# Clustered attention with a max-out FFN on one Trainium2 core: preparations and weight conversion pinned to fixed score tiles, raw weights loaded ahead, value products in one run

## The chip, the cores and the metric

The kernel runs on one core of a Trainium2 chip. Five engines work from queues of their own, each strictly in the order in which its instructions were written: TensorE (PE, matmuls; PEld are its weight loads), VectorE (DVE), ScalarE (ACT), GpSimd (POOL) and SyncE (SP), which here issues every DMA. The metric is device microseconds of one execution. Three runs of the kernel before took 872.66, 874.25 and 877.45 us; the median is 874.25 us.

## The reference

Two steps follow each other. The first is attention that is allowed only inside a cluster, for 4 batches, 8 heads, 768 positions and a head width of 64:

```
q_assign = argmax(q_n @ c_n.T)          # 16 centroids per head, normalised
k_assign = argmax(k_n @ c_n.T)
scores   = q @ k.T / sqrt(64)
scores   = where(q_assign == k_assign, scores, -1e9)
attn     = exp(scores - max) / (sum + 1e-9)
x        = attn @ v                     # then 3072 tokens x 512
h        = max(x @ w1, x @ w2, x @ w3)  # 512 -> 768
out      = h @ w_out                    # 768 -> 512
```

The inputs of the attention are float32 and the four weight matrices are float64. The kernel keeps about float32 accuracy from 16-bit matmuls: an operand is scaled by a power of two and split into a high and a low float16 half, and a product is three matmuls (high by high, high by low, low by high).

## The kernel before, in words

**Tiles.** A *score tile* is 128 query positions of one head against all 768 keys. A batch has 8 heads of 6 tiles, so 48 tiles, and the whole kernel 192, numbered 0 to 191 here. Two heads make a pair (4 pairs a batch), and three tiles of both heads of a pair make a *visit* of six tiles; after the four visits of one half of the queries (24 tiles) come those of the other half.

**One score tile** (`scores`): PE multiplies queries and keys into one of three PSUM buffers `big` (L482 and L484; the second also adds the mask, carried as 32 extra rows of the operands). DVE scales it and takes the row extreme (L487). ACT takes the exponential (L490) and casts it to float16 (L493). The low half is a subtraction (L495), by DVE on even tiles and by POOL on odd ones. On an even tile the whole sequence works in the PSUM buffer, so that the buffer comes free only after the subtraction of DVE; on an odd tile it is free after the exponential. SP then issues a transposing DMA `pt<-hl` (L496).

**One visit** ends with `av`: 6 small matmuls spread the row sums (L510), 36 matmuls of 64 output columns multiply the transposed tiles `pt` with the values (L514), ACT copies the row sums, DVE multiplies (L524, L526), POOL splits the result `x` (L528, L529).

**The FFN** of each half batch (`ffn_units`) has 18 groups of 12 matmuls (L555) and 3 groups of 18 (L589), spread over the 24 tiles that follow. The last half batch has no tiles after it.

**Preparations.** For each pair `prep_units` gives six units: load of two heads, scales, split, cluster scores on PE, moves by DMA, and the argmax with the mask rows on DVE (L434 to L465). `v_prep` splits the values of a pair; batch 0 takes them from two large loads (`v_max_first`), later batches load them inside `v_prep` (L333).

**Weights.** They are float64 in memory. `convert` takes one of two buffers `wd`, loads 512 KB of raw bits (L195), lets ACT cast the high part (L197) and DVE join the low part (L199). There are 18 such pieces for w1, w2, w3 and 6 for w_out, all in batch 0. `split16` then makes the halves. Each load is held back by a tiny POOL copy (`hold`, L120) into the buffer, which reads the row sum of the newest tile.

**What sets the order.** The order of each engine is fixed when the program is built. Every unit gets a priority (`at_prio`), mostly the number of the tile beside which it should stand; a scheduler then fills each engine's queue with a timeline of its own and takes, among what it believes ready, the lowest priority. So a unit whose inputs the scheduler believes ready early is drawn forward into any gap of its timeline. `behind` ties a unit's instructions to one earlier instruction of the same engine; `spread` distributes units over a stretch of tiles.

## Time and profile before

The profiled execution took 872.91 us; its span, from the first to the last instruction, is 871.1 us.

| stretch | us | what is in it |
|---|---|---|
| 0 to 24.8 | 24.8 | start, centroids, preparation of pair 0 |
| 24.8 to 256.6 | 231.8 | tiles 0 to 47: batch 0, all weights |
| 256.6 to 452.2 | 195.6 | tiles 48 to 95: batch 1 |
| 452.2 to 635.9 | 183.7 | tiles 96 to 143: batch 2 |
| 635.9 to 804.8 | 168.9 | tiles 144 to 191: batch 3, nothing left to prepare |
| 804.8 to 871.1 | 66.3 | the last FFN |

The stretches are cut where L487 of tiles 0, 48, 96, 144 and 191 starts. Over the span PE is busy 84%, DVE 64%, ACT 53% and POOL 52%. A matmul's busy time overlaps that of the next one, so that the spacing of starts says what it costs. A timeline row gives the start, the duration, the engine, the line and the tiles, and in brackets how long the engine stood idle before it and what ended that. A row of waits gives the engine and line that waited, for what, the total in us, how many times and the longest.

### The profile page before, as it was taken

To read this page: it belongs to the slowest core of one execution; us is meant where nothing else is said; L and a number is where in the kernel's file an instruction comes from. 1 tells how busy PE (TensorE), PEld (TensorE's weight loads), DVE (VectorE), ACT (ScalarE), POOL (GpSimd) and SP (SyncE) were. 2 spreads that over 40 slices of the span, in tenths; PEclk is the share of its full clock that TensorE was granted. 3 is DMA by queue.
4 is the path that set the end of the run, shared out by engine and by line. 5 is a ranking of instruction groups with operands and counts; after the bars stand their busy time and mean duration, and the time that the engine had idled before them with its cause. 6 is when DMAs were issued, how large, how long until landed. Compare 5 with 4: busy or idle time off the path is not lost.

```text
span 871.1 us, 13288 instructions
## 1 busy us (share of the span) xinstructions
PE 729.3 (84%) x4629; PEld 391.6 (45%) x4629; DVE 559.7 (64%) x1169; ACT 463.1 (53%) x827; POOL 450.4 (52%) x464
## 2 busy tenths in 40 slices
PE   2035374788868989999789999997999999999997
PEld 0012132344434545555444555454545554555563
DVE  7663877786897867547686686368768663556110
ACT  2545467654663646646554656464556465566201
POOL 1166355658585565337655745266666652354221
PEclk9976566689888999999999999999999999999999
DMA  6176869986786778768888978597986976666300
GB/s 230 36 169 140 201 143 214 203 182 139 178 204 128 171 167 154 138 117 165 170 157 201 188 139 142 113 180 144 189 194 128 156 136 134 112 118 110 91 1 36
DMA packets 329154, 128.90 MB, mean 148 GB/s; under 512 B 304384, under 2 KB 315520, under 8 KB 329088
## 3 DMA queue, kind: packets, MB, share of 16 engines
q1 hardware_dynamic: 329088, 128.06, 71.5%
q8 instruction: 36, 0.59, 0.3%
q14 instruction: 30, 0.25, 0.1%
HBM read 31.49 MB, written 6.29 MB: 43 GB/s over the span
## 4 chain that ended last, share of the span: by engine, by line
PE 45%; DVE 18%; POOL 11%; DMA 10%; issue 9%; ACT 5%; SPq 1%; POOLq 0%; DVEq 0%; ACTq 0%
PE one L555 17%; PE one L589 11%; PE big L514 7%; DVE big L487 4%; PE big L482 4%; PE big L484 3%; POOL hl L495 3%; DMA pt<-hl 2%; DMA stage<-in_qk_dram 2%; PE big L510 2%; DMA wd<-in_moe_w_dram 2%; DMA wd<-in_moe_w_out_dram 2%; POOL qk L399 2%; DMA stage<-in_v_dram 2%; DVE hl L495 2%
## 5 line engine op out<-in xcount | busy, mean ns | idle before, releaser
L487 DVE TENSOR_SCALAR_CACHE_REDUCE big<-big,nsc 128x768 f32<-128x768 f32 x192 | 194.2, 1017 | 78.3 <-PE big L484 77.1
L495 POOL TENSOR_TENSOR hl<-e,hl 128x768 f16<-128x768 f32 x96 | 159.0, 1656 | 148.9 <-ACT hl L493 147.3
L555 PE MATMUL one<-x,w16a 128*128 128x384 f16 x1152 | 208.1, 330 | 5.1 <-DVE vf_h L567 3.7
L490 ACT ACTIVATE big<-big,nm 128x768 f32<-128x768 f32 x96 | 83.8, 873 | 146.3 <-DVE big L487 130.9
L555 PEld LDWEIGHTS <-w16a 128*128 128x128 f16 x1152 | 111.1, 98 | 90.0 <-issue 21.1
L482 PE MATMUL big<-qk 128*128 128x512 f16 (+1 forms) x384 | 105.9, 357 | 48.5 <-DVE hl L495 14.0
L514 PE MATMUL big<-pt,v 128*64 128x384 f16 x1152 | 129.8, 341 | 2.4 <-DMA pt<-hl 2.4
L490 ACT ACTIVATE e<-big,nm 128x768 f32<-128x768 f32 x96 | 86.5, 901 | 71.3 <-DVE big L487 56.4
L495 DVE TENSOR_TENSOR hl<-big,hl 128x768 f16<-128x768 f32 x96 | 91.4, 952 | 41.8 <-ACT hl L493 39.6
L555 PE MATMUL one<-x,w16b 128*128 128x384 f16 x576 | 108.3, 340 | 6.7 <-DVE vf_h L567 5.2
L484 PE MATMUL big<-qk 96*128 96x512 f16 (+1 forms) x384 | 106.5, 357 | 6.9 <-DVE qk L465 4.3
L514 PEld LDWEIGHTS <-v 128*64 128x64 f16 x1152 | 71.8, 114 | 50.9 <-issue 26.0
L482 PEld LDWEIGHTS <-qk 128*128 128x128 f16 x384 | 35.6, 102 | 104.8 <-issue 67.2
L493 ACT CAST hl<-e 128x768 f16<-128x768 f32 x96 | 80.1, 834 | 2.4 <-DMA pt<-hl 0.6
L555 PEld LDWEIGHTS <-w16b 128*128 128x128 f16 x576 | 57.5, 101 | 51.3 <-issue 17.5
L493 ACT CAST hl<-big 128x768 f16<-128x768 f32 x96 | 76.6, 798 | 2.0
L528 POOL TENSOR_SCALAR x<-xs 128x384 f16<-128x384 f32 x32 | 16.4, 512 | 99.3 <-DVE xs L524 83.8
L484 PEld LDWEIGHTS <-qk 96*128 96x128 f16 x384 | 40.4, 105 | 40.0 <-issue 9.2
L589 PE MATMUL one<-wo,wf_h 128*128 128x512 f16 x216 | 56.0, 381 | 0.8 <-ACT o L598 0.8
L589 PE MATMUL one<-wo,vf_h 128*128 128x512 f16 x216 | 51.8, 380 | 2.7 <-DVE vf_h L567 2.4
L367 DVE TENSOR_REDUCE q_m<-stage 128x1 f32<-128x768 f32 x32 | 30.2, 948 | 33.9 <-DMA stage<-in_qk_dram 33.8
L399 POOL TENSOR_TENSOR qk<-stage,qk 128x768 f16<-128x768 f32 x30 | 49.6, 1667 | 3.1 <-ACT qk L398 2.9
(150 smaller groups left out, 892.5 us busy)
## 6 DMA issues: line engine op xcount, KB each, us to landing
stage<-in_qk_dram SPq DMA_DIRECT2D x32, 384.0 KB, 5.0
wd<-in_moe_w_dram SPq DMA_DIRECT2D x18, 512.0 KB, 4.8
out_dram<-o SPq DMA_DIRECT2D x24, 256.0 KB, 2.5
qk<-qk SPq DMA_DIRECT2D x15, 384.0 KB, 4.3
qk<-qk SPq DMA_DIRECT2D x30, 192.0 KB, 3.4
stage<-in_v_dram SPq DMA_DIRECT2D x12, 384.0 KB, 4.6
pt<-hl SPq DMA_TRANSPOSE x192, 4.0
wd<-in_moe_w_out_dram SPq DMA_DIRECT2D x6, 512.0 KB, 4.5
```

The costliest lines, as they stand in the source:

```text
L367: nc.vector.tensor_reduce(m2[:, i : i + 1], x, axis=AX.X, op=ALU.max, apply_absolute_value=True)
L399: last["lo"] = nc.gpsimd.tensor_tensor(t[:, AQ, i], x, t[:, BQ, i], op=ALU.subtract)
L482: nc.tensor.matmul(t[:, lo:hi], aq[:, qs], ak[:, lo:hi], start=True, stop=False)
L484: last["pe"] = nc.tensor.matmul(t[:, lo:hi], bq[0:K2, qs], bk[0:K2, lo:hi], start=False, stop=True)
L487: last["nm"] = nc.vector.tensor_scalar(e, e, nsc[b, h // 2], 3.0e38, op0=ALU.mult, op1=ALU.min, accum_out=nm)
L490: nc.scalar.activation(x, e, AF.Exp, bias=nm, scale=-1.0, accum_out=r)
L493: nc.scalar.copy(hl[:, 0, :], x)
L495: eng.tensor_tensor(hl[:, 1, :], x, hl[:, 0, :], op=ALU.subtract)
L510: nc.tensor.matmul(t[D * i : D * i + D, at : at + P], w, ident, start=True, stop=True)
L514: nc.tensor.matmul(t[D * i : D * i + D, 0:NB], v[:, i, kt, a], pts[i][:, :, c * QT + kt, :], start=(n == 0), stop=(n == len(parts) - 1),)
L555: nc.tensor.matmul(t[:, 0:NB], w16[jt // JA][:, jt % JA, wa, i, ct], x16[b, gi, ct][:, xa, :], start=(n == 0), stop=(n == 3 * CT - 1),)
L589: nc.tensor.matmul(t[:, 0:DM], h16[jt][:, ha, tt * P : (tt + 1) * P], wo16[0][:, jt, wa, :], start=(n == 0), stop=(n == 3 * JT - 1),)
```

## The change

Seven edits go together.

- `convert` becomes `w_load` (the DMA) and `w_convert` (ACT and DVE). The `hold` copies on POOL go.
- The 24 raw loads, conversions and splits get fixed tiles: piece n is converted at 1.9 n − 0.8 and loaded two tiles before that; before, they were spread over three stretches.
- `paced` is new: all instructions of a unit are tied behind the newest score matmul (PE), scaling (DVE), exponential (ACT), subtraction (POOL) and transposition (SP) at the point where the plan places it. Preparations, values and weights all go through it, and the raw loads of the later batches' values (`v_load`) stand two tiles ahead of their use.
- The value products are paced too, with a priority five tiles ahead of their place. `AV_LAG` goes from 2 to 3, and what follows the products (`x_split`) is a unit of its own one tile later.
- The two large value loads of batch 0 are issued at the start, and both their maxima are taken beside tiles, not before tile 0.
- `v_prep` of batch 0 stands at tiles 3, 9, 15 and 21.
- The FFN's 18 groups start one tile later in each half batch.

```
+    def w_load(wp, src, a, n):
         x = wp.tile([P, n + 1, 4], I16, tag="wd", name="wd", bufs=2)
-        hold(x[0:1, 0, 0:2].bitcast(F32))
         xf = x.rearrange("p n w -> p (n w)")
         nc.sync.dma_start(out=xf[:, 1 : 1 + 4 * n].rearrange("p (a m) -> p a m", a=a), in_=src)
+        return x
+
+    def w_convert(x, d):
...
-        nc.scalar.activation(x, e, AF.Exp, bias=nm, scale=-1.0, accum_out=r)
-        pace[:] = [r[0:1]]
+        last["exp"] = nc.scalar.activation(x, e, AF.Exp, bias=nm, scale=-1.0, accum_out=r)
...
+        if by_pool:
+            last["pool"] = i
...
+    def paced(step, u, late=-1):
+
+        def f():
+            with ExitStack() as st:
+                for k in ("pe", "nm", "exp", "pool", "dma"):
+                    if k in last:
+                        st.enter_context(tc.issue_after(last[k].ins))
+                u()
+
+        plan.setdefault(max(int(step // 1), 0), []).append((step + late, f))
...
-    behind("lo", vm[0])
+    wl[0]()
     first[5]()
...
-    spread([lambda u=u: behind("nm", u) for u in prep_units(0, 1)], 0, 3, -4)
-    spread([lambda u=u: behind("nm", u) for u in vm[1:]] + [lambda: v_prep(0, 0, True)], 0, 4, 0)
-    spread(prep_units(0, 2), 4, 9, -4)
-    spread(prep_units(0, 3), 10, 15, -4)
+    W_STEP = 1.9
+    for n in range(24):
+        k = 2 + (n - 2) * W_STEP
+        if n >= 2:
+            paced(k - 1, (wl + ol)[n])
+        paced(max(k + 1, 0.5), (wc + oc)[n])
+        if n < 18 and n % 3 == 2:
+            for i, u in enumerate(wu[n // 3][2]):
+                paced(k + 2 + i, u)
+    paced(47, w_common)
+    for k, u in zip((0, 1, 2, 2, 3), p1[1:]):
+        paced(k, u)
+    for k in (2, 3, 4):
+        paced(k - 1, vm[k])
+    prep_at(0, 2, (3, 5, 6, 7, 8, 9))
+    prep_at(0, 3, (9, 11, 12, 13, 14, 15))
+    for pr in range(NPAIR):
+        paced(V * pr + 3, lambda pr=pr: v_prep(0, pr, True))
...
-    spread(wa[W_0:], *W_A, W_LATE)
-    spread([u for j in range(JA, JT) for u in w_units(fp[0], j)], *W_B, W_LATE)
-    spread(wo_units(fp), *W_O, W_LATE)
...
-                t = at + HS + V + 7.5 * pr
-                spread(prep_units(b + 1, pr), t + 1, t + 10, PREP_LATE)
-                t = at + nsteps + (-14, -8, -2, 3)[pr]
-                spread([lambda b=b, pr=pr: v_prep(b + 1, pr)], t, t)
+                t = at + 28 + 9 * pr
+                prep_at(b + 1, pr, (t, t + 2, t + 3, t + 5, t + 6, t + 7))
+                t = at + nsteps + (-13, -7, -1, 3)[pr]
+                paced(t - 2, lambda b=b, pr=pr: v_load(b + 1, pr))
+                paced(t, lambda b=b, pr=pr: v_prep(b + 1, pr))
...
-                spread([u for j in h for u in j], k + 3, k + HS, F_LATE)
+                spread([u for j in h for u in j], k + 4, k + HS, F_LATE)
...
-        u = lambda a=(b, pr, gi, pts, rs): behind("pe", av, *a)
-        plan.setdefault(step + AV_LAG - 1, []).append((step + AV_LATE, u))
+        paced(step + AV_LAG - 1, lambda a=(b, pr, gi, pts, rs): av(*a), -5)
+        paced(step + AV_LAG, lambda a=(b, pr, gi): x_split(*a))
```

The queues of the built programs show three places. Line numbers move with the change: L482, L484, L490, L493, L496, L510, L514, L555, L195 and L197 become L498, L500, L506, L508, L513, L528, L532, L577, L186 and L193.

On PE, a value product of batch 1 (`v_2390` is the split values of pair 3). Before, the products stand between the matmuls of the FFN's output (L589):

```order
L510 MATMUL big<-ident,rs 64x128
L589 LDWEIGHTS wf_h
L589 MATMUL one<-wo_1015,wf_h 128x512
L514 LDWEIGHTS v_2390
L514 MATMUL big<-pt,v_2390 64x384
L589 LDWEIGHTS wf_h
L589 MATMUL one<-wo_1015,wf_h 128x512
```

The same product (there `v_2364`) after the change:

```order
L577 MATMUL one<-x_3086,w16a 128x384
L528 MATMUL big<-ident,rs 64x128 x6
L532 LDWEIGHTS v_2364
L532 MATMUL big<-pt,v_2364 64x384
L532 LDWEIGHTS v_2364
L532 MATMUL big<-pt,v_2364 64x384
```

All 36 products of this visit now follow each other, and score matmuls come next. Counted over the whole queue of PE, a matmul of 64 output columns (L510, L514 and the cluster scores) and one of 128 follow each other 316 times before and 182 times now; from tile 48 on 260 times before and 142 now.

On ACT, tiles 1 and 2 before (`vf` holds the raw values of batch 0, `v_` their split, `stage` and `qk` the preparation of a pair, `wd` raw weights):

```order
L490 ACTIVATE e,rs<-big,nm 128x768
L493 CAST hl<-e 128x768
L330 ACTIVATE vf<-vf,s_v_301 128x768 x2
L397 ACTIVATE stage<-stage,q_s 128x768 x2
L330 ACTIVATE vf<-vf,s_v_301 128x768 x2
L340 CAST v_337<-vf 128x12x64
L340 CAST v_406<-vf 128x12x64
L398 CAST qk<-stage 128x768 x2
L340 CAST v_621<-vf 128x12x64
L340 CAST v_827<-vf 128x12x64
L490 ACTIVATE big,rs<-big,nm 128x768
```

Tiles 1 to 3 now:

```order
L506 ACTIVATE e,rs<-big,nm 128x768
L508 CAST hl<-e 128x768
L506 ACTIVATE big,rs<-big,nm 128x768
L508 CAST hl<-big 128x768
L193 CAST top<-wd 128x512
L413 ACTIVATE stage<-stage,q_s 128x768 x2
L414 CAST qk<-stage 128x768 x2
L506 ACTIVATE e,rs<-big,nm 128x768
```

The twelve instructions that stood between tiles 1 and 2 are apart now; the values of the four pairs follow tiles 5, 9, 15 and 21.

On SP, raw weights between transpositions (`pt_`), around tiles 18 to 22 before:

```order
L496 DMA_TRANSPOSE pt_859<-hl_868 128x12x128
L195 DMA wd_955<-in_moe_w1_dram 128x4x512
L496 DMA_TRANSPOSE pt_859<-hl_884 128x12x128
L195 DMA wd_974<-in_moe_w2_dram 128x4x512
L496 DMA_TRANSPOSE pt_859<-hl_950 128x12x128
L195 DMA wd_991<-in_moe_w3_dram 128x4x512
```

And around tiles 16 to 18 now:

```order
L513 DMA_TRANSPOSE pt_771<-hl_829 128x12x128
L186 DMA wd_839<-in_moe_w2_dram 128x4x512
L513 DMA_TRANSPOSE pt_771<-hl_850 128x12x128
L479 DMA qk_675<-cl_t_797 32x768 x4
L513 DMA_TRANSPOSE pt_858<-hl_867 128x12x128
L186 DMA wd_876<-in_moe_w3_dram 128x4x512
```

The loads keep a transposition or two between them, and no load waits for a POOL copy any more.

More of the change, by code (lines that the diff above doesn't have):

```diff
@@ L112, in pow2_scale @@
         return p, s
-    pace = []
-    def hold(x):
-        if pace:
-            nc.gpsimd.tensor_copy(x, pace[-1])
     last = {}
@@ L243, in split, with load, f @@
             return f
-        return [load(i) for i in range(3)] + [scale] + [split(i) for i in range(3)]
+        return [load(i) for i in range(3)], [conv(i) for i in range(3)], [scale] + [split(i) for i in range(3)]
     def wo_units(fp):
         got = []
+        raw = {}
+        def load(jt):
+            def f():
+                w = w_out.bitcast(I16)[jt * P : (jt + 1) * P, :]
+                raw[jt] = w_load(fp[0], w.rearrange("p (a n) -> p a n", a=1), 1, DM)
+            return f
         def part(jt):
             def f():
-                wp = fp[0]
-                w = w_out.bitcast(I16)[jt * P : (jt + 1) * P, :]
                 if jt % 3 == 0:
-                    got[:] = [wp.tile([P, 3 * DM], F32, tag="wf", name="wf", bufs=2)]
+                    got[:] = [fp[0].tile([P, 3 * DM], F32, tag="wf", name="wf", bufs=2)]
                 x = got[0][:, jt % 3 * DM : (jt % 3 + 1) * DM]
-                convert(wp, w.rearrange("p (a n) -> p a n", a=1), 1, x)
+                w_convert(raw.pop(jt), x)
                 row = worow[:, jt : jt + 1]
@@ L283, in common @@
             wsc["w"], wsc["o"] = pw, po
-        return [part(jt) for jt in range(JT)] + [common]
+        return [load(jt) for jt in range(JT)], [part(jt) for jt in range(JT)], common
     vmax = cpool.tile([P, B, NPAIR], F32, name="vmax")
@@ L308, in v_max_first, with load @@
     def v_max_first():
+        def load(i):
+            x = v_first[i] = fp[0].tile([P, 2 * S], F32, tag="vf", name="vf", bufs=2)
+            h = H // 2
+            nc.sync.dma_start(out=x, in_=vv[0, :, i * h : (i + 1) * h].rearrange("p h t d -> p (h t d)"))
         def part(i):
             def f():
-                x = v_first[i] = fp[0].tile([P, 2 * S], F32, tag="vf", name="vf", bufs=2)
-                h = H // 2
-                nc.sync.dma_start(out=x, in_=vv[0, :, i * h : (i + 1) * h].rearrange("p h t d -> p (h t d)"))
+                x = v_first[i]
                 nc.vector.tensor_reduce(
@@ L321, in sc, with v_load @@
             vsc[0] = pow2_scale(vmax[:, 0, 0:2], "v0")
-        return [part(0), part(1), sc]
+        return [lambda: load(0), lambda: load(1), part(0), part(1), sc]
     v16 = {}
+    v_in = {}
+    def v_load(b, pr):
+        x = v_in[b, pr] = stage()
+        nc.sync.dma_start(out=x, in_=vv[b, :, 2 * pr : 2 * pr + 2].rearrange("p h t d -> p (h t d)"))
     def v_prep(b, pr, loaded=False):
@@ L331, in v_prep @@
         else:
-            x = stage()
-            nc.sync.dma_start(out=x, in_=vv[b, :, 2 * pr : 2 * pr + 2].rearrange("p h t d -> p (h t d)"))
+            x = v_in.pop((b, pr))
             m = vmax[:, b, pr : pr + 1]
@@ L645, in at_prio @@
         u(*args)
+    wu = [w_units(fp[0], j) for j in range(JT)]
+    wl = [u for j in range(JT) for u in wu[j][0]]
+    wc = [u for j in range(JT) for u in wu[j][1]]
+    ol, oc, w_common = wo_units(fp)
     c_sb = load_centroids()
@@ L653, with prep_at @@
         u()
[L654 removed]
+    wl[0]()
     first[5]()
[L656 to L675 removed]
+    p1 = prep_units(0, 1)
+    p1[0]()
+    vm[0]()
+    vm[1]()
+    wl[1]()
+    def prep_at(b, pr, steps):
+        for k, u in zip(steps, prep_units(b, pr)):
+            paced(k, u)
[10 more added lines that the diff above has]
+    for k, u in zip((0, 1, 2, 2, 3), p1[1:]):
+        paced(k, u)
+    for k in (2, 3, 4):
[4 more added lines that the diff above has]
+        paced(V * pr + 3, lambda pr=pr: v_prep(0, pr, True))
+    spread([open_late], LATE, LATE)
     for b in range(B):
```

37 lines of the change are left out of this document (15 added, 22 removed).

## The prediction

> **What bounds the kernel now.** I read the page first: span, PE's use and clock over the 40 slices.
>
> ```profile
> span 871.1 us, 13288 instructions
> PE   2035374788868989999789999997999999999997
> PEclk9976566689888999999999999999999999999999
> ```
>
> From the fourteenth slice on (280 us) PE is nearly always busy at the full clock. Before that it is not, and its clock is down to about half. The stretches between tiles 0, 48, 96, 144 and 191 say the same in numbers (PE, PEld, DVE, ACT and POOL busy, then PE's granted clock, DMA share and GB/s):
>
> ```profile
> 24.80:256.60 231.80, 138.77 (x772) 70.39 (x771) 169.45 (x353) 135.72 (x233) 136.53 (x141) 0.76 0.76 166
> 256.60:452.20 195.60, 179.83 (x1183) 97.40 (x1183) 135.08 (x301) 106.28 (x192) 107.84 (x100) 0.97 0.78 154
> 452.20:635.90 183.70, 175.37 (x1157) 94.97 (x1157) 123.84 (x264) 106.03 (x194) 104.08 (x97) 0.98 0.81 161
> 635.90:804.80 168.90, 168.56 (x1138) 93.47 (x1137) 103.77 (x198) 99.19 (x182) 85.34 (x80) 1.00 0.73 137
> ```
>
> Batch 0 takes 63 us more than batch 3, and no engine fills it: DVE is busiest, and idle for 231.80 − 169.45 = 62.4 us. Batches 2 and 3 are PE's. So I need two things: what DVE waits for in batch 0, and what PE loses later. The waits of DVE between 24 and 257 us:
>
> ```profile
> DVE big L487 <- PE big L484: 25.2, 14, 9.4
> DVE wf L199 <- ACT top L197: 20.3, 12, 3.6
> DVE q_m L367 <- DMA stage<-in_qk_dram: 5.7, 4, 3.4
> ```
>
> L199 joins the low part of the weights and waits for the cast L197, and the cast waits for its load:
>
> ```profile
> 242.21 0.53 SPq L195 DMA_DIRECT2D wd<-in_moe_w_out_dram  x1
> 248.38 0.78 ACT L197 CAST top<-wd 128x512 f16<-128x512 bf16 x1 [1.48 <-DMA wd<-in_moe_w_out_dram]
> 249.19 0.99 DVE L199 SCALAR_TENSOR_TENSOR wf<-wd,top 128x512 int32<-128x512 int32 x1 [1.07 <-ACT top L197]
> ```
>
> The DMA issues (line, count, size, median us to landing) have the load's own time:
>
> ```profile
> wd<-in_moe_w_dram SPq DMA_DIRECT2D x18, 512.0 KB, 4.8
> ...
> qk<-cl_t SPq DMA_DIRECT2D x60, 48.0 KB, 2.0
> ```
>
> The load goes out at 242.21 and the cast starts 6.2 us later, on its landing, with DVE behind. The load went out late because `hold` tied it to row sums; its landing alone takes a median 4.8 us. The longest of the 25.2 us is the clump of twelve ACT instructions after tile 1:
>
> ```profile
> 36.58 1.76 ACT L330 ACTIVATE vf<-vf,s_v 128x768 f32<-128x768 f32 x2 [2.10 <-DVE s_v L111]
> 44.47 1.56 ACT L340 CAST v<-vf 128x768 f16<-128x768 f32 x2
> 45.98 1.03 DVE L487 TENSOR_SCALAR_CACHE_REDUCE big<-big,nsc 128x768 f32<-128x768 f32 x1 [9.38 <-PE big L484]
> ```
>
> PE's later loss is in a timeline of batch 2, where the output matmuls L589 and the value products L514 alternate:
>
> ```profile
> 541.18 0.49 PE L484 MATMUL big<-qk 96*128 96x512 f16 x2
> 541.51 4.26 PE L589 MATMUL one<-wo,wf_h 128*128 128x512 f16 x19
> 545.62 0.49 PE L482 MATMUL big<-qk 128*128 128x512 f16 x2
> ...
> 551.41 0.35 PE L514 MATMUL big<-pt,v 128*64 128x384 f16 x1
> 551.70 0.39 PE L589 MATMUL one<-wo,wf_h 128*128 128x512 f16 x1
> ...
> 557.12 0.39 PE L589 MATMUL one<-wo,wf_h 128*128 128x512 f16 x1
> 557.44 2.30 PE L514 MATMUL big<-pt,v 128*64 128x384 f16 x26
> 559.67 0.34 PE L555 MATMUL one<-x,w16a 128*128 128x384 f16 x1
> ```
>
> In a run, 19 of L589 take 545.62 − 541.51 = 4.11 us, 0.216 each, and 26 of L514 take 2.23 us, 0.086 each: 0.302 for one of both. From 551.41 to 557.44 stand ten alternating pairs, 0.603 each. So each of the two changes of width in a pair costs 0.15 us.
>
> **The change part by part**, against the profiled run's own 872.9 us, which is 1.3 below the median of the runs, so that either base gives the same within the noise.
>
> *Start, −1.75.* A maximum over `vf` (one of two) leaves the chain ahead of tile 0:
>
> ```profile
> L314 DVE TENSOR_REDUCE vmax<-vf 128x1 f32<-128x1536 f32 x2 | 3.5, 1747 | 0.0
> ```
>
> It comes back on DVE beside the tiles, +1.75 in batch 0.
>
> *Weights in batch 0, −14.3.* A load now stands behind the transposition of tile k−1 and its cast behind the exponential of tile k+1.
>
> ```profile
> L490 ACT ACTIVATE big<-big,nm 128x768 f32<-128x768 f32 x96 | 83.8, 873 | 146.3 <-DVE big L487 130.9
> L493 ACT CAST hl<-big 128x768 f16<-128x768 f32 x96 | 76.6, 798 | 2.0
> L495 DVE TENSOR_TENSOR hl<-big,hl 128x768 f16<-128x768 f32 x96 | 91.4, 952 | 41.8 <-ACT hl L493 39.6
> ```
>
> Two tiles are 2 × 231.8/48 = 9.7 us. The transposition goes out at least 0.87 + 0.80 + 0.95 = 2.6 us after its tile's scaling, with SP's own issues perhaps 4.5, the cast about 1 us after its tile's: some 6 us of lead against 4.8. That is on time with little to spare; of the 20.3 us I keep 6. Bounds: none removed, or all. The 22 `hold` copies on POOL cost nothing either way: POOL is idle 95 us there.
>
> *Other loads, −4.6* of the 5.7 us for queries and keys, which are loaded two tiles ahead too (0 to −5.7).
>
> *The clump, −9.4.* Those twelve instructions are spread over tiles 2 to 21, where ACT has 231.8 − 135.7 = 96 us idle; were that cover gone they would cost their roughly 11 us again. The score tiles' PSUM buffers then circulate from the start (−4 to −12).
>
> *Mask rows, +3.3.* The last DVE step of pair 3's preparation stood behind tile 15, and now stands behind tile 17, right ahead of the first tile that needs it: the DMAs of rows (`qk<-cl_t`, 2.0 us to landing) and one tile's scores at a half clock (1.3 us) become visible (0 to +7, if other pairs do the same).
>
> *Changes of width, −15.* From tile 48 on they fall from 260 to 142 in the queue: 118 × 0.15 = 17.7 us. In batch 1 PE is busy 179.8 of 195.6 us and does not always set the end, so I take 15. Below stands 8, if the trace's worst pairs overstate the mean; above 20, with the 16 fewer ahead of tile 48.
>
> *Later batches' loads, −3.* In batch 1 DVE waits for loads:
>
> ```profile
> DVE q_m L367 <- DMA stage<-in_qk_dram: 12.8, 5, 3.3
> DVE vmax L335 <- DMA stage<-in_v_dram: 4.8, 4, 1.9
> ```
>
> DVE is not the bound there; PE's idle 15.8 us is the most that can come back (0 to −10).
>
> *A lean stretch, +5.* The FFN starts one tile later, and its groups bunch: L555 stands 84 times beside tiles 102 to 107 before and 36 times now, with 48 becoming 84 beside the next six.
>
> ```profile
> 823.49 31.36 PE one L555 x192
> ```
>
> At 31.36/192 = 0.163 us, 48 × 0.163 = 7.8 us of PE's work goes out of that stretch in each of batches 1 to 3. DVE and ACT work through the tiles meanwhile, and only what PE stands idle is lost: 0 to 23 us in all. I take 5, near the lower end, since the next stretch is fuller by as much and the PSUM buffers decouple three tiles.
>
> *Subtractions later on DVE, +3.* The pinned units push L495 back: summing the rows' durations, DVE's work between an even tile's L487 and its L495 goes from 2.40 to 2.69 us on the mean, 28 us over 96 tiles.
>
> ```profile
> PE big L482 <- DVE hl L495: 14.0, 8, 8.2
> ```
>
> PE waited for it on 8 of 96, so a twelfth of 28 counts (0 to 28).
>
> Sum: −1.75 + 1.75 − 14.3 − 4.6 − 9.4 + 3.3 − 15 − 3 + 5 + 3 = −35, so **838 us**. Batch 0 then takes about 209 us. The DMA engines were busy 0.76 × 231.8 = 176 us in it and move the same bytes, a share of 0.84; 0.91 was reached between 150 and 200 us (below), so they allow it.
>
> **The rivals.**
>
> *More comes back, 806 us.* With the loads out of the way DVE could run batch 0 at 90%: (169.45 + 1.75)/0.9 = 190 us, −42; with all 17.7 of the width changes, 1.75 at the start and 6 of the later loads −67. For it: PE and DVE hold over 90% later. Against: the DMA share would have to be 0.93.
>
> *The change does not do what it says, 857 us.* The lead of 6 us is worked out from means. All loads share one SP queue with the transpositions, and if those stand in it, cast and load meet again: neither 14.3 nor 4.6 comes, leaving −16.
>
> *PE starves and loses its clock, slower.* Its clock falls where PE has gaps:
>
> ```profile
> 50.00:100.00 50.00, 18.22 (x93) 8.08 (x91) 31.11 (x65) 23.28 (x38) 26.32 (x26) 0.62 0.78 177
> 150.00:200.00 50.00, 36.89 (x212) 20.01 (x213) 38.12 (x75) 30.00 (x56) 32.59 (x38) 0.76 0.91 188
> 600.00:650.00 50.00, 44.22 (x265) 22.47 (x264) 35.03 (x80) 30.21 (x53) 33.36 (x30) 0.93 0.83 169
> ```
>
> The now leaner tiles (54 to 59 and 78 to 89 of a batch's span, and the same places in batches 2 and 3) hold some 46 us of PE work per batch at the full clock (18 tiles of scores at twice the 0.33 us from 541.18 to 541.51, 138 of L555 at 0.163, three visits' products with their row sums at nearly 4). At 0.62 they take 74 us, against some 54 us of DVE work beside them: +20 a batch, 60 in all, 898 us. It decides from 35/3 = 11.7 us a batch, a clock of 46/(54 + 11.7) = 0.70 there. For it: the rows show 0.62 with PE at 36%. Against: at 44.2 of 50 us it was still 0.93, and in the lean tiles PE still has 46 us of work in 54.
>
> [...]
>
> **How the numbers follow.** The forecast has 0.56, its own range 820 to 856. More comes back: 0.16. The loads stay late: 0.14. The clock: 0.14, of which a milder form that only eats the gain has 0.04. A change under 0.5% (4.4 us) is called none; that is about what a measurement of this kernel can tell. Faster is all of the first three but for 0.02 that ends within 0.5%, so 0.84; the same 0.06; slower 0.10. The range is 806 to 868: it takes in the greater gain and the late loads, and leaves out the clock's cases and the tails.
>
> **What would show it.** Of the profile after: the row of L199 with about 6 us behind L197 and not 20.3; no wait of 9 us at tile 2; batch 0 (tile 0 to 48) in about 209 us; timelines of the later batches with L514 in one run of 36, and batches 2 and 3 some 5 us shorter each; PE's clock at 0.95 or more from tile 48 on. The forecast is wrong if batch 0 stays over 225 us, if batches 2 and 3 do not shorten, or if the loads are late again.

## The result, and the profile after

The changed kernel takes **947.5 us** (median of four runs, 944.6 to 952.4) against 873.45 us for the kernel before on the same chip: 1.085 times as long, 95% interval 1.078 to 1.091. The forecast was 838 us, 806 to 868; it was wrong in sign. The profiled run of the changed kernel took 945.69 us.

The page of the changed kernel: span, PE's busy time and its share, PE's use and granted clock over the 40 slices.

```profile
span 943.6 us, 13225 instructions
...
PE 721.6 (76%) x4629; PEld 398.0 (42%) x4629; DVE 565.8 (60%) x1169; ACT 460.7 (49%) x827; POOL 450.5 (48%) x442
...
PE   3224425687669789978769799986969799899898
...
PEclk9956556888888989979789999989979899999999
```

The same row of the kernel before:

```profile
PE 729.3 (84%) x4629; PEld 391.6 (45%) x4629; DVE 559.7 (64%) x1169; ACT 463.1 (53%) x827; POOL 450.4 (52%) x464
```

PE works 7.7 us less than before and stands idle 80 us more (943.6 − 721.6 = 222.0 against 871.1 − 729.3 = 141.8). So most of the loss is PE waiting. The 7.7 us hides a smaller part: the order now has 134 fewer changes of width (316 against 182), which at the 0.18 us each that g5 below gives would take some 24 us off PE's work. By this estimate some 16 us came back, at a granted clock of 0.90, 0.93 and 0.96 in batches 1 to 3, where it was 0.97, 0.98 and 1.00. Where before PE was nearly full from the fourteenth slice on, it now has holes of a tenth to four tenths to the end.

The stretches between tiles 0, 48, 96, 144, 191 and the end (us; then PE, PEld, DVE, ACT and POOL busy, PE's granted clock, DMA share, GB/s):

```profile
22.30:274.50 252.20, 134.40 (x798) 70.36 (x797) 171.64 (x355) 135.82 (x235) 139.79 (x123) 0.74 0.69 153
274.50:482.90 208.40, 178.00 (x1157) 98.90 (x1157) 134.28 (x284) 105.12 (x190) 104.52 (x97) 0.90 0.73 140
482.90:689.80 206.90, 175.61 (x1156) 97.59 (x1156) 127.32 (x264) 105.02 (x190) 104.75 (x97) 0.93 0.73 142
689.80:880.40 190.60, 172.87 (x1168) 98.13 (x1168) 107.61 (x215) 101.13 (x186) 85.95 (x81) 0.96 0.69 131
```

Against 231.8, 195.6, 183.7 and 168.9 before, every batch loses 13 to 23 us, batch 3 as much as the others, though it has no weights and only its own last two preparations reach into it. In batch 3 PE was busy 168.56 of 168.9 us at clock 1.00; now it is busy 172.87 of 190.6 at 0.96.

The waits of the changed kernel over the whole run (engine and line that waited, for what; total us, times, longest):

```profile
ACT xs L540 <- PE big L532: 117.3, 29, 7.8
...
PEld L388 <- DVE q_m L386: 43.6, 8, 10.1
...
PE big L528 <- DVE rs L523: 21.9, 10, 6.1
...
DVE wf L195 <- ACT top L193: 21.0, 12, 4.9
...
DVE q_m L383 <- DMA stage<-in_qk_dram: 19.7, 14, 3.2
...
PE big L500 <- DMA qk<-cl_t: 18.8, 3, 8.6
```

L388 is the scaling matmul of a preparation (before: L372), L528 the row sums ahead of the value products (L510), L540 the copy behind them (L522). Two things stand out. PE, the engine that sets the end, now waits for preparations and for inverse row sums. And the wait that was to go, DVE's at the join of the weights, is still there: 21.0 us, before 20.3.

A timeline of batch 3, tiles 156 to 159 (start, duration, engine, line; in brackets the idle time before and what ended it):

```profile
746.09 0.29 PE L388 MATMUL one<-ident,q_m 128*128 128x128 bf16 x1 [3.07 <-DVE q_m L386]
746.17 7.22 PE L577 MATMUL one<-x,w16a 128*128 128x384 f16 x32
...
755.73 0.49 PE L500 MATMUL big<-qk 96*128 96x512 f16 x2
...
756.55 1.02 DVE L503 TENSOR_SCALAR_CACHE_REDUCE big<-big,nsc 128x768 f32<-128x768 f32 x1
...
759.75 2.94 PE L577 MATMUL one<-x,w16a 128*128 128x384 f16 x17
...
762.61 0.88 PE L528 MATMUL big<-ident,rs 128*64 128x128 f32 x12
...
763.32 3.10 PE L532 MATMUL big<-pt,v 128*64 128x384 f16 x36
...
766.48 0.48 ACT L540 COPY xs<-big 128x384 f32<-128x384 f32 x1 [4.73 <-PE big L532]
...
767.21 1.03 DVE L503 TENSOR_SCALAR_CACHE_REDUCE big<-big,nsc 128x768 f32<-128x768 f32 x1 [0.23 <-PE big L500]
```

The 36 value products do stand in one run, as forecast. But between the scalings (L503) of tiles 158 and 159, the third and the fourth of a visit, lie 10.7 us: FFN matmuls, row sums and the whole run are queued between the two tiles' scores, and ACT stands at its copy. This repeats in every visit: on the mean, without the first visit of each batch, 10.1 us lie between third and fourth tile in batch 3, 4.6 before (9.9 to 12.0 against 4.0 to 5.9 in the other batches).

### The profile page after: what moved, and what is told of

Same layout as the page of the kernel before. It is cut to its first block, busy times and chain, and to the rows that moved or that the text cites. A ratio compares the mean times of both kernels' runs of the same rounds, so it can differ in the third digit from the quotient of the medians.

```text
span 943.6 us, 13225 instructions
## 1 busy us (share of the span) xinstructions
PE 721.6 (76%) x4629; PEld 398.0 (42%) x4629; DVE 565.8 (60%) x1169; ACT 460.7 (49%) x827; POOL 450.5 (48%) x442
## 4 chain that ended last, share of the span: by engine, by line
PE 46%; DVE 15%; DMA 14%; issue 8%; POOL 7%; ACT 5%; SPq 4%; POOLq 0%; DVEq 0%; ACTq 0%
PE one L577 20%; PE one L611 9%; PE big L532 7%; DVE big L503 5%; DMA stage<-in_qk_dram 4%; DMA qk<-qk 3%; PE big L500 3%; PE big L498 3%; DMA wd<-in_moe_w_dram 2%; POOL hl L510 2%; DMA pt<-hl 2%; SPq L513 2%; ACT hl L508 2%; PE big L528 2%; DVE q_m L383 2%
## 5 line engine op out<-in xcount | busy, mean ns | idle before, releaser
L510 POOL TENSOR_TENSOR hl<-e,hl 128x768 f16<-128x768 f32 x96 | 157.9, 1645 | 306.6 <-ACT hl L508 296.4
L503 DVE TENSOR_SCALAR_CACHE_REDUCE big<-big,nsc 128x768 f32<-128x768 f32 x192 | 192.6, 1021 | 146.4 <-PE big L500 132.8
L577 PE MATMUL one<-x,w16a 128*128 128x384 f16 x1152 | 214.6, 343 | 8.9 <-POOL x L550 7.7
L577 PEld LDWEIGHTS <-w16a 128*128 128x128 f16 x1152 | 116.1, 102 | 94.9 <-issue 30.1
L498 PE MATMUL big<-qk 128*128 128x512 f16 (+1 forms) x384 | 100.7, 347 | 54.9 <-ACT e L506 18.2
L506 ACT ACTIVATE e<-big,nm 128x768 f32<-128x768 f32 x96 | 86.5, 901 | 95.5 <-DVE big L503 82.0
L532 PE MATMUL big<-pt,v 128*64 128x384 f16 x1152 | 117.1, 358 | 6.2 <-DMA pt<-hl 6.2
L506 ACT ACTIVATE big<-big,nm 128x768 f32<-128x768 f32 x96 | 84.0, 875 | 75.6 <-DVE big L503 71.6
L500 PE MATMUL big<-qk 96*128 96x512 f16 (+1 forms) x384 | 101.5, 349 | 22.5 <-DMA qk<-cl_t 18.8
L510 DVE TENSOR_TENSOR hl<-big,hl 128x768 f16<-128x768 f32 x96 | 91.3, 952 | 29.9 <-ACT hl L508 29.7
L577 PE MATMUL one<-x,w16b 128*128 128x384 f16 x576 | 98.1, 326 | 1.2 <-DVE w_s L273 0.6
L532 PEld LDWEIGHTS <-v 128*64 128x64 f16 x1152 | 75.4, 122 | 40.8 <-issue 6.5
L498 PEld LDWEIGHTS <-qk 128*128 128x128 f16 x384 | 34.5, 100 | 113.5 <-issue 67.9
L508 ACT CAST hl<-e 128x768 f16<-128x768 f32 x96 | 79.9, 832 | 1.1
L508 ACT CAST hl<-big 128x768 f16<-128x768 f32 x96 | 76.7, 799 | 0.9
L540 ACT COPY xs<-big 128x384 f32<-128x384 f32 x32 | 15.3, 477 | 117.3 <-PE big L532 117.3
L577 PEld LDWEIGHTS <-w16b 128*128 128x128 f16 x576 | 55.8, 98 | 39.5 <-issue 3.0
L500 PEld LDWEIGHTS <-qk 96*128 96x128 f16 x384 | 39.0, 102 | 53.2 <-DMA qk<-cl_t 17.9
L589 DVE SCALAR_TENSOR_TENSOR wf_h<-one,wf_h 128x384 f32<-128x384 f32 x48 | 26.6, 553 | 48.6 <-PE one L577 42.9
L528 PE MATMUL big<-ident,rs 128*64 128x128 f32 x384 | 34.3, 324 | 27.3 <-DVE rs L523 21.9
```

Source lines behind the costliest of these rows:

```text
L498: nc.tensor.matmul(t[:, lo:hi], aq[:, qs], ak[:, lo:hi], start=True, stop=False)
L500: last["pe"] = nc.tensor.matmul(t[:, lo:hi], bq[0:K2, qs], bk[0:K2, lo:hi], start=False, stop=True)
L503: last["nm"] = nc.vector.tensor_scalar(e, e, nsc[b, h // 2], 3.0e38, op0=ALU.mult, op1=ALU.min, accum_out=nm)
L506: last["exp"] = nc.scalar.activation(x, e, AF.Exp, bias=nm, scale=-1.0, accum_out=r)
L508: nc.scalar.copy(hl[:, 0, :], x)
L510: i = eng.tensor_tensor(hl[:, 1, :], x, hl[:, 0, :], op=ALU.subtract)
```

## The experiments

Each stands against runs of the kernel before on the same chip. Its median there is 869 to 873 us, depending on the chip, so what a change costs in us is worked out from the ratios. Two theories at the start: V, the value products cost the time (the gap in each visit, and batch 3's loss); P, the pinned preparations and weights cost it (the waits at L388).

### The parts one by one

e1 is before with the new value products and the FFN one tile later:

```diff
-        u = lambda a=(b, pr, gi, pts, rs): behind("pe", av, *a)
-        plan.setdefault(step + AV_LAG - 1, []).append((step + AV_LATE, u))
+        paced(step + AV_LAG - 1, lambda a=(b, pr, gi, pts, rs): av(*a), -5)
+        paced(step + AV_LAG, lambda a=(b, pr, gi): x_split(*a))
```

> The kernel before with only the new value products (paced behind tile S+2 of the next visit, put three tiles ahead in the order, copy L540 in one run with them, division one tile later) and the FFN one tile later, which they need. Theory V (the value products cost it): in the changed kernel batch 3, which has hardly any preparations and no weights, lost 190.6 - 168.9 = 21.7 us; four batches of about 21 less 3 at the end give 873 + 81 = about 955 us here, with some 10 us between the third and the fourth tile of each visit. Theory P (the pinned preparations, weights and loads cost it): nothing changes for the worse, 855 to 873 us, the lower end if the changes of width are worth 15 us.

e3 is before with the pinned preparations of batches 1 to 3, their value loads and value splits:

```diff
-                t = at + HS + V + 7.5 * pr
-                spread(prep_units(b + 1, pr), t + 1, t + 10, PREP_LATE)
-                t = at + nsteps + (-14, -8, -2, 3)[pr]
-                spread([lambda b=b, pr=pr: v_prep(b + 1, pr)], t, t)
...
+                t = at + 28 + 9 * pr
+                prep_at(b + 1, pr, (t, t + 2, t + 3, t + 5, t + 6, t + 7))
+                t = at + nsteps + (-13, -7, -1, 3)[pr]
+                paced(t - 2, lambda b=b, pr=pr: v_load(b + 1, pr))
+                paced(t, lambda b=b, pr=pr: v_prep(b + 1, pr))
```

> The kernel before with only the preparations of batches 1 to 3 and the value loads at fixed tiles. Theory V: 865 to 880 us, since the table of stretches puts the loss into batch 3 as well. Theory P: batches 0 to 2 (each prepares the next) lose up to 20 us each by PE's wait for q_m at its matmul (43.6 us in the changed kernel against 9.8): 900 to 930 us.

e4 is before with the start, the weights and batch 0's preparations as changed:

> The kernel before with only the weights, loads and preparations of batch 0 at fixed tiles (the start included). Theory V: batch 0 gains what was forecast of it, 16 to 25 us, so 850 to 860 us. Theory P: batch 0 loses some 20 us of the changed kernel's, 885 to 895 us.

e5 is the changed kernel with the value products of before:

```diff
-        paced(step + AV_LAG - 1, lambda a=(b, pr, gi, pts, rs): av(*a), -5)
-        paced(step + AV_LAG, lambda a=(b, pr, gi): x_split(*a))
+        u = lambda a=(b, pr, gi, pts, rs): behind("pe", av, *a)
+        plan.setdefault(step + AV_LAG - 1, []).append((step + AV_LATE, u))
```

> The changed kernel with the value products as before (behind the newest scores on PE alone, at their old place in the order, copy and division with them), FFN still one tile later. Theory V: the loss is gone and the rest of the forecast comes, 845 to 870 us. Theory P: 930 to 950 us, as the changed kernel.

| kernel | us, median | ratio to before (95%) | start | batch 0 | 1 | 2 | 3 | end |
|---|---|---|---|---|---|---|---|---|
| before | 869.4 | 1 | 24.8 | 231.8 | 195.6 | 183.7 | 169.0 | 66.3 |
| changed | 947.5 | 1.085 (1.078–1.091) | 22.3 | 252.2 | 208.4 | 206.8 | 190.7 | 63.1 |
| e1, values | 896.4 | 1.031 (1.027–1.035) | 24.4 | 238.5 | 198.1 | 203.2 | 168.3 | 63.2 |
| e3, preparations | 932.6 | 1.073 (1.068–1.078) | 24.6 | 237.9 | 205.8 | 211.1 | 184.7 | 66.3 |
| e4, start and weights | 875.8 | 1.007 (1.004–1.009) | 22.4 | 242.6 | 189.3 | 184.7 | 169.1 | 66.3 |
| e5, all but values | 951.9 | 1.095 (1.091–1.099) | 22.4 | 240.8 | 215.9 | 212.9 | 187.8 | 70.5 |

(The stretches are those of each profiled run.) V fell as the main cause: e5, without the new value products, is no faster than the changed kernel, and e1 loses nothing in batch 3, although its gap there is 9.0 us. The gap of one visit is made up in its other tiles. Of P the part on the preparations holds, 64 us alone (7.3% of 869.4), and the part on the weights does not, 6 us. The parts alone add to 27 + 64 + 6 = 97 us, more than the 74 of all together. None of the four fell inside a range that either theory had put down for it; e3 and e5 missed P's by 2 to 3 us.

Batch 3 loses 15.7 us in e3, though only the preparations of its pairs 2 and 3 (steps 142 to 158) and the values of the same pairs reach into it. From tile 174 on e3 takes what before takes. Tiles 144 to 174 before, then in e3:

```profile
635.90:748.80 112.90, 112.56 (x732) 60.40 (x731) 70.80 (x139) 65.44 (x120) 59.66 (x55) 1.00 0.72 141
```

```profile
679.40:808.10 128.70, 117.85 (x734) 62.66 (x735) 76.78 (x155) 66.89 (x122) 59.17 (x53) 0.93 0.67 138
```

PE does the same work there, 732 and 734 matmuls. It stands idle 128.70 − 117.85 = 10.9 us where it stood 0.3, and the same matmuls keep it busy 5.3 us longer, at a clock of 0.93. Tile by tile the loss shows in 156 to 162, which take 16.1 us more. That stretch before, then in e3:

```profile
686.90:702.80 15.90, 15.90 (x121) 9.52 (x120) 13.77 (x24) 8.46 (x15) 8.63 (x9) 1.00 0.72 136
```

```profile
735.10:767.10 32.00, 30.82 (x192) 16.85 (x193) 19.98 (x40) 16.68 (x32) 17.86 (x16) 0.90 0.58 112
```

In that stretch itself PE is busy 30.82 of 32.00 us: 71 matmuls that stood elsewhere before now fall into it. The idle time lies mostly ahead, 5.2 us in tiles 144 to 149 and 4.5 in 150 to 155. The timeline of e3 there (L372 to L386 scale a pair, L400 to L404 split it, L428 is the first cluster matmul, L487 and L489 are scores, L562 the FFN's first matrices):

```profile
715.05 4.06 PE L562 MATMUL one<-x,w16a 128*128 128x384 f16 x24
...
731.64 0.49 PE L489 MATMUL big<-qk 96*128 96x512 f16 x2
...
735.00 0.21 DVE L374 TENSOR_SCALAR q_m<-q_m 128x1 f32<-128x1 f32 x1
...
736.28 0.29 PE L377 MATMUL one<-ident,q_m 128*128 128x128 bf16 x1 [4.15 <-DVE q_m L375]
736.36 6.63 PE L562 MATMUL one<-x,w16a 128*128 128x384 f16 x24
...
739.67 1.79 POOL L400 TENSOR_SCALAR stage<-stage,q_s 128x768 f32<-128x768 f32 x2 [0.31 <-DVE q_s L384]
740.61 0.83 ACT L403 CAST qk<-stage 128x768 f16<-128x768 f32 x1 [1.15 <-POOL stage L400]
...
742.93 0.40 PE L428 MATMUL big<-qk,cw 128*64 128x512 f16 x1
743.26 0.50 PE L487 MATMUL big<-qk 128*128 128x512 f16 x2
```

The scaling matmul L377 stands at the head of PE's queue for 4.15 us, for its input on DVE, which in that time scales three tiles at 1.02 us each (L492); 24 FFN matmuls that then run at once stand behind it. After it, PE has those 24 and then the cluster matmul, which needs the rest of the chain: DVE, POOL, ACT, 6.6 us. The next scores stand behind that. From 731.64 to 743.26 no tile gets scores; 6.6 of these 11.6 us go to FFN matmuls that have to be done in any case.

The tile that had last begun when a pair's reductions (L367, e3 L372), its scaling matmul and its first cluster matmul started, for the four preparations of batch 3, worked out from the starts in each trace:

| pair | before | e3 | f5 | f3 | f6 |
|---|---|---|---|---|---|
| 0 | 98, 128, 131 | 127, 129, 129 | 123, 126, 128 | 99, 126, 129 | 129, 131, 131 |
| 1 | 107, 133, 138 | 136, 138, 138 | 135, 136, 138 | 132, 136, 138 | 136, 139, 139 |
| 2 | 133, 143, 146 | 145, 147, 147 | 141, 144, 147 | 145, 147, 147 | 145, 146, 146 |
| 3 | 146, 151, 153 | 153, 156, 156 | 151, 153, 155 | 147, 152, 156 | 151, 153, 154 |

Before, the scheduler drew the reductions up to 30 tiles ahead, and 2 to 5 tiles' scores stood between scaling and cluster matmul. Pinned, scaling and cluster matmul fall beside one tile. PE's wait for the scaling matmul's input, in batches 1 to 3 of e3:

```profile
PE one L377 <- DVE q_m L375: 35.6, 5, 10.9
```

Before, PE has no such wait there. In these three batches PE stands idle 69.0 us in e3 and 24.4 before, so that this one wait is as much as four fifths of the difference.

### What of the preparations costs it

f5 is e3 with the first half of the chain three tiles earlier; f3 is e3 without the ties of the preparations (the value loads and splits keep theirs); f6 is before with the preparations' ties only, at its own tiles and priorities:

```diff
-                prep_at(b + 1, pr, (t, t + 2, t + 3, t + 5, t + 6, t + 7))
+                prep_at(b + 1, pr, (t - 3, t - 1, t, t + 5, t + 6, t + 7))
```

> The pinned preparations alone (as in e3), with load, scaling and split three tiles earlier and the cluster scores, moves and rows where they were; in PE's queue 1 to 3 score tiles then stand between the scaling matmul and the first cluster matmul of most pairs, where in e3 none did. Theory C (the loss is the chain's latency: scaling matmul, DVE, POOL, ACT, cluster matmul, with no tile between): of the 63 us lost in e3 some 40 come back, 885 to 900. Theory T (the ties themselves cost it, wherever they are): 925 to 940. Theory L (the loads, two tiles ahead, are late): 925 to 940 too, since the load keeps its two tiles.

```diff
-            paced(k, u)
+            plan.setdefault(k, []).append((k - 1, u))
```

> The pinned preparations alone (as in e3), at the same tiles and priorities but tied to no instruction, so that the scheduler may draw steps forward. The scaling matmul then stands 3 to 4 tiles ahead of the first cluster matmul for three of four pairs, 0 for the third. Theory C: 880 to 900 us. Theory T: 870 to 875, all of the 63 back. If the place alone (five tiles for a chain that had 30) costs it: 920 to 935.

```diff
-                spread(prep_units(b + 1, pr), t + 1, t + 10, PREP_LATE)
+                for i, u in enumerate(prep_units(b + 1, pr)):
+                    paced(t + 1 + 1.5 * i, u, PREP_LATE)
```

> The kernel before with only the preparations of batches 1 to 3 tied behind the newest tile's instructions, at the tiles and priorities they already had. In PE's queue the scaling matmul, which stood 2 to 5 tiles ahead of the first cluster matmul, now stands beside the same tile as it for nearly every pair: the ties hold it back, not the place. Theory T (the ties are some 35 of the 63 us that e3 lost, its other tiles the 28 that f3 lost): 895 to 915 us, with scores standing still for some 8 us between the two matmuls. If only the new places cost time: 865 to 880.

f5 took 915.5 us, 1.054 (1.049–1.058); f3 898.8, 1.033 (1.029–1.038); f6 937.6, 1.078 (1.074–1.081). So the ties alone do all of the damage, 67 us, at the tiles and priorities of before, and more than had been expected of f6: they keep the scheduler from drawing the steps forward (the reductions of pair 0 stand beside tile 98 before, beside 129 in f6).

The 29 us of f3 belong to the new places and to the tied value loads and splits together. In batches 1 to 3 of f3 PE waits 13.9 us for inverse row sums (0.5 before) and 9.2 us for the scale of a pair's values (L106, none before), and idles 21 us more. The second wait is the values' own. No run took their ties away.

Three tiles more between the halves (f5) give back 17 of e3's 64 us, less than the theory of the chain's latency (40) expected. PE's wait for the scaling matmul's input is gone in f5, but PE waits 39.2 us for exponentials that free a score buffer, 14.8 in e3. And in f6 two waits of PE are of one size; the first was 2.4 us in the kernel before, the second was not there:

```profile
PE big L516 <- DMA pt<-hl: 21.1, 8, 5.3
PE one L372 <- DVE q_m L370: 20.6, 6, 6.6
```

So the wait at the scaling matmul is the largest that e3 shows, but with it gone most of the loss stays: the ties cost time in other ways too. What holds back the exponentials in f5 and the transposed tiles in f6 was not taken apart.

f7, f9 and f10 are e3 with the preparations tied on some engines alone; f7 is shown, and the value loads and splits keep all their ties:

```diff
-            paced(k, u)
+            def f(u=u):
+                with ExitStack() as st:
+                    for n in ('pe',):
+                        if n in last:
+                            st.enter_context(tc.issue_after(last[n].ins))
+                    u()
+
+            plan.setdefault(k, []).append((k - 1, f))
```

> The pinned preparations of batches 1 to 3 (as in e3), tied on PE alone. PE's queue has almost the order of f3, which was tied to nothing (898.75 us; scaling matmul 3 to 4 tiles ahead of the cluster scores for three of four pairs). Theory D (the ties on DVE, which hold the reductions and with them the scaling matmul's input, cost it): as f3, 893 to 905 us. Theory Q (PE's own tie costs it: a waiting matmul at the head of its queue): 920 to 935.

> The same, tied on DVE alone. The two reductions and the scaling matmul fall back to where e3 had them (scaling matmul 0 to 3 tiles ahead of the cluster scores). Theory D: as e3, 920 to 940 us. Theory Q: 893 to 905.

> The pinned preparations of batches 1 to 3 (as in e3) tied on ACT and POOL alone. Tied to nothing they cost 28 us, tied on DVE 39, tied everywhere 63. If the ties on ACT and POOL are the rest (22 us beyond DVE's): 915 to 925. If it is the ties together, each holding back the next step of one chain: 898 to 908.

f7 took 900.9 us, 1.034 (1.028–1.040); f9 (`"nm"` alone) 910.0, 1.043 (1.038–1.047); f10 (`"exp"` and `"pool"`) 901.8, 1.035 (1.030–1.041). PE's own tie costs nothing that can be measured beyond f3, as theory D said, though PE is where the waits show; ACT's and POOL's cost at most a few us. DVE's costs 8 us beyond f3, which is less than D expected. Of the 34 us between f3 and e3, some 24 need either the tie on SP (loads, moves and mask rows behind transpositions) or ties on several engines together. That f10 fell into the range put down for ties that cost time only together speaks for the second; no run ties them on SP alone, and it stays open.

### The value products

g1 is e1 with the tie on PE alone; g5 is before with one number changed.

```diff
-        paced(step + AV_LAG - 1, lambda a=(b, pr, gi, pts, rs): av(*a), -5)
+        plan.setdefault(step + AV_LAG - 1, []).append(
+            (step + AV_LAG - 6, lambda a=(b, pr, gi, pts, rs): behind("pe", av, *a)))
```

> The value products alone (as in e1), still in a run and tied behind the newest scores on PE, but no longer tied on ACT, DVE, POOL and SP, so that the inverse of the row sums may be taken as soon as they are there. Theory I (in e1 PE waits for that inverse, 30.2 us in 9 waits, and ACT then for the run): the 27 us lost in e1 come back, 860 to 872 us, or 850 if PE's shorter work counts. Theory R (some 68 matmuls between two tiles' scores starve DVE and ACT whatever they wait for): 890 to 900.

```diff
-    W_LATE, F_LATE, AV_LATE = -2, 0, 2
+    W_LATE, F_LATE, AV_LATE = -2, 0, -3
```

> The kernel before with one number changed: the value products five tiles further ahead in the order, so that they stand in runs (188 changes of width in PE's queue instead of 316), tied and placed as before. By the term for changes of width in the prediction (0.15 us each): 128 x 0.15 = 19 us less, 850 to 860 us. If a change of width costs PE time that it has anyway: 868 to 875. Theory R: 880 to 895.

g1 took 871.1 us, 1.000 (0.997–1.002); g5 872.8, 1.003 (1.001–1.005). In g1 all 27 us of e1 are back; theory R, that a run of products between two tiles starves DVE and ACT in any case, fell. The waits of e1:

```profile
ACT xs L525 <- PE big L517: 103.9, 24, 7.8
...
PE big L513 <- DVE rs L508: 30.2, 9, 8.8
```

and of g1 the same wait of ACT, and the group of the row sums with its idle time:

```profile
ACT xs L525 <- PE big L517: 63.4, 24, 8.1
```

```profile
L513 PE MATMUL big<-ident,rs 128*64 128x128 f32 x384 | 32.5, 304 | 12.0 <-ACT e L490 6.6 <-DVE rs L508 5.4
```

ACT still waits 63.4 us for the runs (23.5 before), and the time is that of before. PE's wait for the inverse row sums went from 30.2 us in e1 to 5.4, as theory I had it, and these 24.8 are close to the 27 that came back. But the two do not lie in the same place. In batch 0 the wait falls by 18.4 us (23.8 to 5.4), and batch 0 takes 239.3 us in place of 238.5. What comes back is 6.7 us in batch 1 and 21.9 in batch 2, where the wait falls by 3.6 and 2.6. So the ties beyond PE's cost the 27 us, but that they did it by way of this wait is not shown. They were taken away on ACT, DVE, POOL and SP together, so that no one of them is shown to be it either.

g5 tests the term for changes of width, 188 in PE's queue in place of 316. Its page and its batch 3:

```profile
PE 706.3 (81%) x4629; PEld 394.7 (45%) x4629; DVE 559.0 (64%) x1169; ACT 462.0 (53%) x827; POOL 451.6 (52%) x464
```

```profile
641.70:803.70 162.00, 157.37 (x1118) 91.22 (x1116) 103.32 (x194) 99.31 (x183) 83.21 (x77) 1.00 0.78 145
```

PE's busy time falls by 729.3 − 706.3 = 23.0 us, 0.18 for each of the 128 changes; the 0.15 was a fair price. Batch 3, where PE was full, takes 162.0 in place of 169.0. The other batches give nothing, batch 0 takes 4.5 more, the end 1.5, and the whole is no faster.

### The weights, and joining what helped

h1 is e4 with batch 0's preparations of pairs 1 to 3 queued as before; h2 is h1 with the raw weights one tile earlier.

```diff
-    for k, u in zip((0, 1, 2, 2, 3), p1[1:]):
-        paced(k, u)
+    spread([lambda u=u: behind("nm", u) for u in p1[1:]], 0, 3, -4)
...
-    prep_at(0, 2, (3, 5, 6, 7, 8, 9))
-    prep_at(0, 3, (9, 11, 12, 13, 14, 15))
+    spread(prep_units(0, 2), 4, 9, -4)
+    spread(prep_units(0, 3), 10, 15, -4)
```

> The start and the weights of the changed kernel (as in e4), with batch 0's preparations of pairs 1 to 3 queued as before. Theory C (in batch 0 too the pinned preparations ate the weights' gain: PE waited 16.2 us for q_m, 16.8 for mask rows, 16.9 for cluster scores): batch 0 falls from 242.6 to 215 to 225, the time to 848 to 858. If the weights' steps themselves stand in the way: 870 to 878 as in e4.

```diff
-            paced(k - 1, (wl + ol)[n])
+            paced(k - 2, (wl + ol)[n])
```

> h1 with the raw weights loaded three tiles ahead of their conversion in place of two (two buffers still suffice). If the lead is what was too short in the changed kernel, the casts no longer start on the landing, DVE's wait at the join (14.7 us in batch 0 of h1) falls below 6 and batch 0 by about as much: 858 to 864 us. If DVE's wait there has cover (PE or the buffers set batch 0's pace): the wait falls and the time stays, 865 to 870.

h1 took 868.3 us, 0.998 (0.996–1.000): batch 0 falls from 242.6 to 231.1, where it was before the change. So the pinned preparations took 11.5 us in batch 0 too (batch 1 gives 4.8 of it back, 189.3 in e4 and 194.1 in h1), but the weights had no gain of their own for them to eat, and neither range put down for h1 holds. h2 took **856.5 us, 0.980 (0.975–0.985)**, its batch 0 in the profiled run 212.3. That run was the fastest of four (850.7 us); n2 below, with the same loads, has 218.4 there. Batch 0's waits in h1:

```profile
ACT top L193 <- DMA wd<-in_moe_w_dram: 15.7, 10, 2.4
...
DVE wf L195 <- ACT top L193: 14.7, 11, 3.1
```

and in h2, with the stretch:

```profile
DVE wf L195 <- ACT top L193: 9.5, 9, 3.2
...
ACT top L193 <- DMA wd<-in_moe_w_dram: 5.0, 4, 2.5
```

```profile
22.80:235.10 212.30, 130.79 (x784) 67.68 (x783) 167.86 (x350) 134.62 (x236) 136.50 (x120) 0.80 0.83 181
```

From issue to cast lie a median 4.8 us before, 5.2 in the changed kernel and 6.4 in h2, and 4.5 to 4.8 to the landing (worked out over 22 loads of each trace); 17 of 22 casts started within 0.2 us of the landing before, 14 in the changed kernel, 5 in h2. A cast that starts on the landing has waited for it, so that the lead which the order gave it was shorter still. Two tiles of lead were too short by one. The wait of DVE at the join fell by 5 us only, not below 6; ACT's for the loads by 11, and the stretch by 19. What else the earlier loads set free in it was not taken apart.

m1 is before with g1's products from batch 1 on, m3 is before with g5's number from batch 1 on; n1 and n2 are h1 and h2 with m1's products.

> The kernel before with the value products of g1 (in a run, tied on PE alone, division a tile later) from batch 1 on, batch 0 as before. By the stretches of g1 (191.4, 181.3 and 165.8 against 195.6, 183.7 and 169.0, the end 1.5 longer) and of before (batch 0 231.8): 871 - 9 + 1.5, 860 to 866 us. If g1's gain hung on its batch 0: 868 to 873.

> The kernel before with the value products five tiles further ahead in the order from batch 1 on only (as g5, batch 0 as before). By g5's stretches (197.3, 184.0, 162.0, end 67.8): 871 - 3.5, 864 to 870. If the changes of width are worth what the prediction put on them in the batches that PE bounds: 855 to 862.

> h1 (start and weights as changed, preparations as before) with the value products of m1 from batch 1 on. By the stretches: h1's start 22.6 and batch 0 231.1, m1's 191.6, 183.3, 167.3 and 67.8: 863.7 and 1.8 around the span, 862 to 868 us; 858 to 862 if m1's 229.8 for batch 0 is kept with h1's earlier start.

> h2 (start and weights as changed, loads three tiles ahead, preparations as before) with the value products of m1 from batch 1 on. By the stretches: h2's start 22.8 and batch 0 212.3, n1's 189.7, 183.1, 166.5 and 67.8: 842 us of span, 843 to 852 with the spread that h2 showed (850.7 to 858.7). If the runs of value products give nothing on top: 853 to 858.

m1 took 863.9 us, 0.992 (0.990–0.995); m3 866.8, 0.996 (0.993–0.999); n1 861.5, 0.988 (0.984–0.992); n2 **851.1, 0.977 (0.973–0.981)**, the best of all; by the ratios it takes 0.977/1.085 = 0.90 of the changed kernel's time. From n1 to n2 it is again the one tile of lead; n2's and h2's intervals overlap, so that what the products add to h2 is not settled.

## Why the prediction was wrong

**Later batches' loads, −3: the step that failed.** It looked at the pinned preparations of batches 1 to 3 as loads alone, and took at most a gain. They cost 64 us (e3), and their ties without the new places cost 67 (f6). The scaling matmul and the cluster matmul were held back by their ties until they stood beside one tile, where the scheduler had kept 2 to 5 tiles between them, and PE waited out the chain: 35.6 us of the 44.6 that it idles more in batches 1 to 3 of e3. That is the largest wait, not the whole: without it (f5) 47 of the 64 us stay lost, and how the ties cost those stays open. That the preparations of before were drawn far forward was to be seen in the order of PE and DVE: the distance between two steps of one chain, counted in tiles of scores. The prediction compared single places and never that distance. `paced` was costed by what it makes late on its own engine, and not by the next engine's step that needs it.

**Weights in batch 0, −14.3: right in kind, the lead too short.** "Some 6 us of lead against 4.8" was 5.2 us, with 14 of 22 casts waiting for the landing. Tiles come in bursts: two of them took from 1.9 to 20.3 us in that batch (starts of L503), where the prediction used 9.7 throughout. With one tile more the whole kernel gains 2%, and batch 0 took 212.3 us in h2's profile and 218.4 in n2's, where 209 were forecast. The rival in which the loads stay late described this part; its 857 us fell with the preparations.

**Changes of width, −15: the price right, the place wrong.** 0.18 us each against 0.15 put down, yet only batch 3 turned PE's shorter work into time (7 us). In batches 0 to 2 PE has idle time that takes it up. A lone busy engine was taken for the bound in stretches where a wait sets the pace.

**The value products' new waits: not in the sum.** They were costed by width alone. Their ties beyond PE's cost 27 us (e1 against g1); PE's wait for the inverse row sums went with them, but is not shown to be what cost the time.

**The clump, −9.4.** The 9.4 us wait is gone, and tile 0 starts 2.5 us earlier (−1.75 forecast). DVE's wait for scores in batch 0 stays at 25.3 us in all (25.2 before); the longest piece is now 4.6. The gain was a wait that moved.

**Mask rows, +3.3.** PE waited 18.8 us for them (3 times, up to 8.6): right mechanism, a sixth of the size. It came three times in batch 0, not once.

**A lean stretch, +5.** In batch 3 of e1, the first tiles of the second half's FFN (168 to 174) take 6.4 us less and the next twelve 6.6 more; the last five take 3.1 more and the end 3.1 less: nothing in all. **Subtractions later, +3**, was not taken apart; PE's wait for L510 is 4.2 us in all.

**The rival that named the sign**, PE starving and losing its clock, put it into the lean tiles by way of the clock. The clock does fall, to 0.90 to 0.96 in batches 1 to 3, but mainly as a consequence of waits. In e3, whose order has nearly as many changes of width as before (288 against 316), PE's busy time rises by 741.8 − 729.3 = 12.5 us and its idle time by 46.8, of 59.3 us of span. So, as an estimate, the clock's own part is about a fifth there. It shows behind a wait: 24 matmuls of L562 took 4.06 us at 715.05, and 6.63 us at 736.36 right behind the wait of 4.15 us; the clock's part at this gap, estimated as the difference of the two, is 2.6 us.

The traces show the granted clock at 0.50 behind shorter waits as well. The stretches ahead of a fall and behind it, first in e3 at the wait of 4.15 us, then in the kernel before at waits of 2.21 and 0.65 us (us, the five engines, PE's granted clock, DMA share, GB/s):

```profile
731.35:734.76 3.41, 0.78 (x4) 0.26 (x3) 3.38 (x5) 1.31 (x2) 2.09 (x2) 1.00 0.59 119
734.76:741.58 6.82, 5.30 (x18) 2.54 (x19) 5.26 (x14) 5.63 (x12) 3.49 (x4) 0.50 0.70 128
```

```profile
604.46:607.87 3.41, 1.16 (x7) 0.60 (x7) 2.82 (x6) 3.24 (x6) 2.99 (x4) 1.00 0.31 66
607.87:611.28 3.41, 3.41 (x13) 1.61 (x11) 3.41 (x11) 3.08 (x7) 3.41 (x4) 0.50 1.06 204
```

The trace of the kernel before has 13 such falls from 1.00 to 0.50, that of the changed kernel 18. In the 3.41 us ahead of each PE stood idle for at least 1.64 us, in one wait or in several: the least was 1.64 us ahead of the fall at 43.37 in the changed kernel, and before 1.77 us ahead of the one at 164.13. As much did not always cost the clock: from 273.36 to 276.77 in the kernel before PE stood idle for 1.91 us, and the granted clock stayed at 1.00.

All three signs given for a failure were seen: batch 0 over 225 us, batches 2 and 3 longer, the loads late again (DVE's wait at the join near 20 us).

## What to carry to other kernels

A tie that pins a step to a tile can cost nothing on the engine where the time is lost, and much by way of the step that this engine waits for: here ties on PE alone cost nothing measurable, and the preparations' ties on all engines 35 us more than none of theirs (e3 against f3). Before pinning a chain, count the tiles of other work that lie between its steps, on the engine that sets the end and on the one that feeds it, before and after. A lead in tiles should be taken from the shortest bursts, not from the mean; here one tile more was worth 2%. And work taken off the busiest engine was worth time only in the batch where that engine had no waits of its own.
